# Attention values multiplied into the up weights batch by batch, nine rows to a partition, and stages interleaved by hand

## The chip, the cores and the metric

The kernel runs on one core of a Trainium2 chip. The metric is the device time of one execution in microseconds (us). Times of stretches and of single instructions come from one profiled execution, taken by the hardware profiler.

## What is computed

Eight batches of a memory attention, 8 heads of 576 tokens and 64 channels, with 32 memory slots a head, followed by a bilinear feed-forward layer over all 4608 tokens (512 channels, 1536 hidden). Cut to what matters:

```python
a = exp(phi - max(phi, axis=2)); a = a / (sum(a, axis=2) + 1e-09)
k_m = einsum('bhsm,bhsd->bhmd', a, k)
v_m = einsum('bhsm,bhsd->bhmd', a, v)
scores = matmul(q, k_m.transpose(0, 1, 3, 2)) / sqrt(64)
attn = softmax(scores, axis=-1)
x = matmul(attn, v_m).transpose(0, 2, 1, 3).reshape(4608, 512)
out = ((x @ w_a) * (x @ w_b)) @ w_out
```

All inputs are float32 in HBM, and so is the output.

## The kernel before

`attention_load(b)` (line 99) loads one batch in five chunks of 128 tokens (the last has 64), each chunk with the tokens on the partitions. phi comes over SP's queue (L113), q, k and v over POOL's queue (L115 to L117), which turns them into float16 on the way; a run in HBM is one token of one head, 64 numbers of q, k or v or 32 of phi. ACT takes the exponential of phi (L120), TensorE transposes q (L124, tile pqTc). Then, for two groups `g` of four heads, TensorE sums exp(phi) times k, v and a column of eights into pkvm (L138), 32 columns of the array to a head, and transposes the key part (L151).

`attention_tail(b)` (line 159) works in blocks of 288 tokens: the scores of four heads in four tiles of the array, 64 rows by 32 columns each (pscore, L168), exponential on ACT (L176), softmax denominators by a matmul with a block matrix (pD, L178), their reciprocals on DVE (L184, two halves of 144, for each block and group), the product (L185), and the values, poutT (L199), copied into `xT_sb`, the attention output of all tokens with the 512 channels on partitions.

`ffn(tbs)` (line 213) takes one or two blocks of 512 tokens. For each of 12 slices of the hidden width it sums four matmuls of 128 x 128 by 512 columns into pa and four into pb (L221), copies pa out on ACT or DVE (L231, L233), and multiplies by pb on DVE (L235). Then po (L240) sums 12 matmuls for each chunk of 128 tokens, which is copied out (L249, L251) and stored over SP's queue (L253).

The order of calls at the end of the function is attention(0), the loads of w_a and w_b (L90, L91), attention(1), attention(2), the load of w_out (L95), ffn([0]), and so on; a scheduler that goes by priorities and the readiness of data moves instructions within it, so attention work of later batches stands between pa and pb matmuls.

Of the kernel before, what the change touches and what calls it, by code (L numbers as in the profile page):

```python
# [8 lines left out]
F32 = mybir.dt.float32  # L10
F16 = mybir.dt.float16
AF = mybir.ActivationFunctionType
ALU = mybir.AluOpType


@with_exitstack
def kernel(
# [11 lines left out]
    nc = tc.nc  # L29
# [3 lines left out]
    d_model, d_ff = moe_w_a.shape  # L33
    T = out.shape[0]

    P = 128
    n_ch = (S + P - 1) // P
    ch_sz = [min(P, S - P * c) for c in range(n_ch)]
    SBK = 288
    n_sbk = S // SBK  # L40
    n_dm = d_model // P
    n_ffc = d_ff // P
    TBLK = 512
    n_tblk = T // TBLK
    KVW = 2 * D + 4
    inv_sqrt_d = 1.0 / float(D) ** 0.5

    consts = ctx.enter_context(tc.tile_pool(name="consts", bufs=1))
    persist = ctx.enter_context(tc.tile_pool(name="persist", bufs=1))
    a_in = ctx.enter_context(tc.tile_pool(name="a_in", bufs=6))  # L50
    ph_pool = ctx.enter_context(tc.tile_pool(name="ph_pool", bufs=3))
    kv_pool = ctx.enter_context(tc.tile_pool(name="kv_pool", bufs=3))
    a_bb = ctx.enter_context(tc.tile_pool(name="a_bb", bufs=3))
    ffn_hp = ctx.enter_context(tc.tile_pool(name="ffn_hp", bufs=3))
    ffn_op = ctx.enter_context(tc.tile_pool(name="ffn_op", bufs=3))
    ps_kvm = ctx.enter_context(tc.tile_pool(name="ps_kvm", bufs=1, space=bass.MemoryType.PSUM))
    ps_rot = ctx.enter_context(tc.tile_pool(name="ps_rot", bufs=3, space=bass.MemoryType.PSUM))
    ps_ab = ctx.enter_context(tc.tile_pool(name="ps_ab", bufs=2, space=bass.MemoryType.PSUM))

    ident16 = consts.tile([P, P], F16, name="ident16")  # L60
    make_identity(nc, ident16)
    blk32 = consts.tile([P, P], F16, name="blk32")
    nc.vector.memset(blk32, 0.0)
    nc.gpsimd.affine_select(
        out=blk32,
        in_=blk32,
        compare_op=ALU.is_gt,
        fill=0.125,
        base=1 - M,
        pattern=[[-M, P // M], [0, M]],  # L70
        channel_multiplier=1,
    )
    nc.gpsimd.affine_select(
        out=blk32,
        in_=blk32,
        compare_op=ALU.is_ge,
        fill=0.0,
        base=0,
        pattern=[[-M, P // M], [0, M]],
        channel_multiplier=1,  # L80
    )

    wa_sb = persist.tile([P, n_dm, d_ff], F16, name="wa_sb")
    wb_sb = persist.tile([P, n_dm, d_ff], F16, name="wb_sb")
    wout_sb = persist.tile([P, n_ffc, d_model], F16, name="wout_sb")
    xT_sb = persist.tile([P, n_dm, T], F16, name="xT_sb")

    def load_weights_ab():
        for c in range(n_dm):
            nc.gpsimd.dma_start(out=wa_sb[:, c, :], in_=moe_w_a[c * P:(c + 1) * P, :])  # L90
            nc.gpsimd.dma_start(out=wb_sb[:, c, :], in_=moe_w_b[c * P:(c + 1) * P, :])  # L91

    def load_weights_out():
        for i in range(n_ffc):
            nc.gpsimd.dma_start(out=wout_sb[:, i, :], in_=moe_w_out[i * P:(i + 1) * P, :])  # L95

    state = {}

    def attention_load(b):
        exp_phi = ph_pool.tile([P, n_ch, H, M], F16, name="exp_phi")  # L100
        qT_sb = a_bb.tile([P, n_dm, S], F16, name="qT_sb")
        kvm_sb = a_bb.tile([P, 2, 2 * D + 1], F16, name="kvm_sb")
        rphi_sb = a_bb.tile([P, 2], F32, name="rphi_sb")
        kmT_sb = a_bb.tile([P, 2, P], F16, name="kmT_sb")
        E_sb = a_bb.tile([P, 2, n_sbk, SBK], F16, name="E_sb")
        kv_b = kv_pool.tile([P, n_ch, H, KVW], F16, name="kv_b")
        state[b] = (qT_sb, kvm_sb, rphi_sb, kmT_sb, E_sb)

        for c in range(n_ch):
            cs = ch_sz[c]  # L110
            s0 = c * P
            phi_ch = a_in.tile([P, H, M], F32, name="phi_ch")
            nc.sync.dma_start(out=phi_ch[:cs], in_=phi[b, :, s0:s0 + cs, :].transpose([1, 0, 2]))  # L113
            q_ch = a_in.tile([P, H, D], F16, name="q_ch")
            nc.gpsimd.dma_start(out=q_ch[:cs], in_=q[b, :, s0:s0 + cs, :].transpose([1, 0, 2]))  # L115
            nc.gpsimd.dma_start(out=kv_b[:cs, c, :, 0:D], in_=k[b, :, s0:s0 + cs, :].transpose([1, 0, 2]))  # L116
            nc.gpsimd.dma_start(out=kv_b[:cs, c, :, D:2 * D], in_=v[b, :, s0:s0 + cs, :].transpose([1, 0, 2]))  # L117
            nc.vector.memset(kv_b[:cs, c, :, 2 * D:2 * D + 1], 8.0)

            nc.scalar.activation(out=exp_phi[:cs, c], in_=phi_ch[:cs], func=AF.Exp)  # L120

            pqTc = ps_rot.tile([P, n_dm, P], F16, name="pqTc", tag="ps_rot")
            for hp in range(n_dm):
                nc.tensor.transpose(  # L124
                    out=pqTc[:, hp, 0:cs],
                    in_=q_ch[:cs, 2 * hp:2 * hp + 2, :],
                    identity=ident16[0:cs, 0:cs],
                    tile_position=(0, 0),
                )
            nc.scalar.copy(out=qT_sb[:, :, s0:s0 + cs], in_=pqTc[:, :, 0:cs])  # L130

        for g in range(2):
            pkvm = ps_kvm.tile([P, KVW], F32, name="pkvm", tag="pkvm")
            for c in range(n_ch):
                cs = ch_sz[c]
                for j in range(4):
                    h = 4 * g + j
                    nc.tensor.matmul(  # L138
                        pkvm[32 * j:32 * (j + 1), 0:2 * D + 1],
                        exp_phi[:cs, c, h, :],  # L140
                        kv_b[:cs, c, h, 0:2 * D + 1],
                        start=(c == 0),
                        stop=(c == n_ch - 1),
                        tile_position=(0, 32 * j),
                    )
            nc.scalar.copy(out=kvm_sb[:, g, :], in_=pkvm[:, 0:2 * D + 1])  # L146
            nc.vector.reciprocal(out=rphi_sb[:, g:g + 1], in_=kvm_sb[:, g, 2 * D:2 * D + 1])  # L147

            pkmT = ps_rot.tile([P, P], F16, name="pkmT", tag="ps_rot")
            for half in range(2):  # L150
                nc.tensor.transpose(  # L151
                    out=pkmT[64 * half:64 * half + 64, :],
                    in_=kvm_sb[:, g, 0:D],
                    identity=ident16[:, :],
                    tile_position=(0, 64 * half),
                )
            nc.scalar.copy(out=kmT_sb[:, g, :], in_=pkmT)

    def attention_tail(b):
        qT_sb, kvm_sb, rphi_sb, kmT_sb, E_sb = state.pop(b)  # L160
        for g in range(2):
            for sb in range(n_sbk):
                pscore = ps_rot.tile([P, SBK], F32, name="pscore", tag="ps_rot")
                for j in range(4):
                    h = 4 * g + j
                    hp = h // 2
                    po2 = 64 * (h % 2)
                    nc.tensor.matmul(  # L168
                        pscore[32 * j:32 * (j + 1), :],
                        kmT_sb[po2:po2 + 64, g, 32 * j:32 * (j + 1)],  # L170
                        qT_sb[po2:po2 + 64, hp, sb * SBK:(sb + 1) * SBK],
                        start=True,
                        stop=True,
                        tile_position=(po2, 32 * j),
                    )
                nc.scalar.activation(out=E_sb[:, g, sb, :], in_=pscore, func=AF.Exp, scale=rphi_sb[:, g:g + 1])  # L176
                pD = ps_rot.tile([P, SBK], F32, name="pD", tag="ps_rot")
                nc.tensor.matmul(pD, blk32, E_sb[:, g, sb, :], start=True, stop=True, tile_position=(0, 0))  # L178
                recipD_sb = a_in.tile([P, SBK], F16, name="recipD_sb")
                HB = SBK // 2  # L180
                for hhh in range(2):
                    sl = slice(hhh * HB, (hhh + 1) * HB)
                    with nc.allow_low_precision("softmax denom reciprocal in fp16 is fine"):
                        nc.vector.reciprocal(out=recipD_sb[:, sl], in_=pD[:, sl])  # L184
                    nc.vector.scalar_tensor_tensor(  # L185
                        out=E_sb[:, g, sb, sl],
                        in0=E_sb[:, g, sb, sl],
                        scalar=rphi_sb[:, g:g + 1],
# [115 lines left out]
```

## Time and profile before

| | |
|---|---|
| median of 3 runs | 418.93 us (418.82 to 419.03) |
| span of the profiled execution | 416.7 us |
| TensorE busy | 346.5 us, 2096 matmuls |
| DVE / ACT / POOL busy | 204.9 / 111.8 / 112.6 us |
| read from HBM, written | 42.47 MB, 9.44 MB |
| mean granted TensorE clock | 0.975 |

PE is TensorE, PEld its weight loads, DVE the vector engine, ACT the scalar engine, POOL and SP the engines that here mostly issue transfers. A row of the groups gives line, engine, operation, output and inputs, count, then busy time and mean duration of one in ns, then the idle time before it and what ended it. Rows of the chain give start, duration and what the program waited for or did; rows of the timeline give start, duration, engine and instruction, with equal neighbours merged. The 40 slices of the page are 10.4 us each. The last two columns of the windows table are the busy share of the DMA engines and GB/s by bytes landed.

### The profile page before, as it was taken

How to read it: one execution, taken by the hardware profiler on the slowest of the kernel's cores; microseconds unless marked ns; L12 is line 12 of the kernel's file. 1: busy time of each engine (PE TensorE's matmuls, PEld its weight loads, DVE VectorE, ACT ScalarE, POOL GpSimd, SP SyncE). 2: the span in 40 equal slices, each digit the busy share in tenths (PEclk: the TensorE clock that was granted, in tenths of full speed). 3: DMA queues.
4: the chain of work that ended last, by engine and by line, in shares of the span. 5: the costliest groups of instructions: out<-in, count | busy, mean ns of one | idle time of the engine just before them, and what ended most of it. 6: DMA issues, size and time to landing. Idle time of an engine off the chain costs nothing.

```text
span 416.7 us, 5430 instructions
## 1 busy us (share of the span) xinstructions
PE 346.5 (83%) x2096; PEld 152.9 (37%) x2096; DVE 204.9 (49%) x391; ACT 111.8 (27%) x255; POOL 112.6 (27%) x148
## 2 busy tenths in 40 slices
PE   0200357994789999999999989999899999999996
PEld 0100113341234444344444434444344444444442
DVE  0000254773551898861198895116965512555411
ACT  3201424562432334311325321115311111111110
POOL 9544526796986913000302000000000000000000
PEclk9999996998689999999999999999999999999999
DMA  9999999999999969002471500220000022000022
GB/s 128 147 200 192 146 146 79 175 187 147 139 154 189 154 39 58 2 0 102 114 46 11 36 0 2 76 101 27 0 2 1 0 102 101 2 0 0 2 101 101
DMA packets 158105, 33.38 MB, mean 80 GB/s; under 512 B 150912, under 2 KB 152448, under 8 KB 158080
## 3 DMA queue, kind: packets, MB, share of 16 engines
q0 software_dynamic: 115392, 18.88, 60.7%
q1 hardware_dynamic: 42688, 14.16, 18.1%
q8 instruction: 16, 0.26, 0.2%
q14 instruction: 9, 0.07, 0.1%
HBM read 42.47 MB, written 9.44 MB: 125 GB/s over the span
## 4 chain that ended last, share of the span: by engine, by line
PE 75%; DMA 13%; ACT 3%; DVE 3%; issue 2%; POOL 1%; SPq 0%; DVEq 0%; POOLq 0%
PE po L240 23%; PE pa L221 22%; PE pb L221 21%; DMA phi_ch<-in_phi_dram 11%; DMA kv_b<-in_v_dram 2%; PE poutT L199 2%; PE pqTc L124 2%; DVE recipD_sb L184 2%; PE pD L178 1%; PE pkvm L138 1%; ACT h_sb L231 1%; PE pscore L168 1%; ACT xT_sb L209 1%; DVE E_sb L185 1%; POOL kv_b L116 1%
## 5 line engine op out<-in xcount | busy, mean ns | idle before, releaser
L221 PE MATMUL pa<-xT_sb,wa_sb 128*128 128x512 f16 x432 | 116.4, 386 | 4.1 <-ACT h_sb L231 3.9
L221 PE MATMUL pb<-xT_sb,wb_sb 128*128 128x512 f16 x432 | 113.1, 385 | 0.0
L240 PE MATMUL po<-wout_sb,h_sb 128*128 128x512 f16 x432 | 96.0, 383 | 0.0
L235 DVE TENSOR_TENSOR h_sb<-h_sb,pb 128x512 f16<-128x512 f16 x108 | 70.7, 681 | 37.0 <-PE pb L221 35.2
L184 DVE RECIPROCAL recipD_sb<-pD 128x144 f16<-128x144 f32 x64 | 63.0, 1026 | 24.6 <-PE pD L178 24.3
L231 ACT CAST h_sb<-pa 128x512 f16<-128x512 f32 x60 | 35.2, 586 | 136.1 <-PE pa L221 136.1
L240 PEld LDWEIGHTS <-h_sb 128*128 128x128 f16 x432 | 42.6, 99 | 52.0 <-issue 2.2
L221 PEld LDWEIGHTS <-wa_sb 128*128 128x128 f16 x432 | 40.9, 99 | 51.2 <-issue 7.2
L115 POOL DMA_DIRECT2D q_ch<-in_q_dram x40 | 34.0, 862 | 94.0 <-PE pqTc L124 84.4
L221 PEld LDWEIGHTS <-wb_sb 128*128 128x128 f16 x432 | 41.2, 98 | 46.9 <-issue 4.2
L251 DVE COPY o_sb<-po 128x512 f32<-128x512 f32 x18 | 12.4, 691 | 78.8 <-PE po L240 78.8
L233 DVE CAST h_sb<-pa 128x512 f16<-128x512 f32 x48 | 33.0, 688 | 19.9 <-PE pa L221 19.8
L116 POOL DMA_DIRECT2D kv_b<-in_k_dram x40 | 35.3, 883 | 7.5 <-DMA wb_sb<-in_moe_w_b_dram 2.4
L124 PE MATMUL pqTc<-ident,q_ch 128*128 128x128 f16 (+1 forms) x160 | 14.6, 233 | 27.3 <-ACT qT_sb L130 18.0
L117 POOL DMA_DIRECT2D kv_b<-in_v_dram x40 | 35.3, 883 | 5.8 <-DMA q_ch<-in_q_dram 2.8
L249 ACT COPY o_sb<-po 128x512 f32<-128x512 f32 x18 | 10.5, 586 | 77.9 <-PE po L240 77.9
L138 PE MATMUL pkvm<-kv_b,exp_phi 128*32 128x129 f16 (+1 forms) x320 | 15.1, 237 | 17.3 <-DMA kv_b<-in_v_dram 16.1
L120 ACT ACTIVATE exp_phi<-phi_ch 128x256 f16<-128x256 f32 (+1 forms) x40 | 15.2, 413 | 37.1 <-DMA phi_ch<-in_phi_dram 37.1
L147 DVE RECIPROCAL rphi_sb<-kvm_sb 128x1 f32<-128x1 f16 x16 | 1.9, 152 | 43.6 <-ACT kvm_sb L146 43.6
L130 ACT COPY qT_sb<-pqTc 128x512 f16<-128x512 f16 (+1 forms) x40 | 19.3, 550 | 14.4 <-PE pqTc L124 14.3
L124 PEld LDWEIGHTS <-q_ch 128*128 128x128 f16 (+1 forms) x160 | 10.8, 105 | 33.1 <-issue 19.9
L138 PEld LDWEIGHTS <-exp_phi 128*32 128x32 f16 (+1 forms) x320 | 7.5, 96 | 34.0 <-issue 22.5
(28 smaller groups left out, 129.4 us busy)
## 6 DMA issues: line engine op xcount, KB each, us to landing
out_dram<-o_sb SPq DMA_DIRECT2D x36, 256.0 KB, 2.0
phi_ch<-in_phi_dram SPq DMA_DIRECT2D x32, 128.0 KB, 8.1
q_ch<-in_q_dram POOLq DMA_DIRECT2D x32, 128.0 KB, 4.7
kv_b<-in_k_dram POOLq DMA_DIRECT2D x32, 128.0 KB, 6.2
kv_b<-in_v_dram POOLq DMA_DIRECT2D x32, 128.0 KB, 6.8
wa_sb<-in_moe_w_a_dram POOLq DMA_DIRECT2D x4, 384.0 KB, 11.0
wb_sb<-in_moe_w_b_dram POOLq DMA_DIRECT2D x4, 384.0 KB, 11.7
wout_sb<-in_moe_w_out_dram POOLq DMA_DIRECT2D x12, 128.0 KB, 5.9
```

The costliest lines, as they stand in the source:

```text
L115: nc.gpsimd.dma_start(out=q_ch[:cs], in_=q[b, :, s0:s0 + cs, :].transpose([1, 0, 2]))
L116: nc.gpsimd.dma_start(out=kv_b[:cs, c, :, 0:D], in_=k[b, :, s0:s0 + cs, :].transpose([1, 0, 2]))
L117: nc.gpsimd.dma_start(out=kv_b[:cs, c, :, D:2 * D], in_=v[b, :, s0:s0 + cs, :].transpose([1, 0, 2]))
L124: nc.tensor.transpose(out=pqTc[:, hp, 0:cs], in_=q_ch[:cs, 2 * hp:2 * hp + 2, :], identity=ident16[0:cs, 0:cs], tile_position=(0, 0),)
L130: nc.scalar.copy(out=qT_sb[:, :, s0:s0 + cs], in_=pqTc[:, :, 0:cs])
L138: nc.tensor.matmul(pkvm[32 * j:32 * (j + 1), 0:2 * D + 1], exp_phi[:cs, c, h, :], kv_b[:cs, c, h, 0:2 * D + 1], start=(c == 0), stop=(c == ...
L184: nc.vector.reciprocal(out=recipD_sb[:, sl], in_=pD[:, sl])
L221: nc.tensor.matmul(pzs[ti], w_sb[:, c, i * P:(i + 1) * P], xT_sb[:, c, tbs[ti] * TBLK:(tbs[ti] + 1) * TBLK], start=(c == 0), stop=(c == n_ ...
L231: nc.scalar.copy(out=h_sbs[ti][:, i, :], in_=pas[ti])
L233: nc.vector.tensor_copy(out=h_sbs[ti][:, i, :], in_=pas[ti])
L235: nc.vector.tensor_tensor(out=h_sbs[ti][:, i, :], in0=h_sbs[ti][:, i, :], in1=pbs[ti], op=ALU.mult)
L240: nc.tensor.matmul(po, h_sbs[ti][:, i, jj * P:(jj + 1) * P], wout_sb[:, i, :], start=(i == 0), stop=(i == n_ffc - 1),)
```

## The change

The kernel is rewritten around the same mathematics. Parts:

1. **Values into the weights.** The attention output x is no longer formed. With A the softmax weights (32 slots x 8 heads = 256 rows by 576 tokens) and V the value memory of one batch, x W = A^T (V W). For every batch the kernel computes V W for both up weights (tiles `vab`, PSUM tile `pva`, L245): 48 matmuls of 64 x 32 weights by 512 columns, four heads in four tiles of the array. The up projection then contracts over 256 rows: per batch, slice and half of the tokens two matmuls of 288 columns into pa (L317) and two into pb (L326).
2. **Nine rows to a partition.** q, k, v and phi of a batch come in one transfer each, all on POOL's queue. A partition holds nine consecutive tokens of a head, one run of 576 numbers (288 of phi). Two heads share the 128 partitions, so the sums over tokens (pkv, L159) run with 64 rows, nine matmuls a head, 192 columns each: k, v and a third block of eights. Softmax denominators of both groups and both halves go to one tile (pD, L214), reciprocals are taken once per batch (2 x 144), and a small matmul spreads them again (pR, L228).
3. **Hand-ordered interleaving.** No scheduler moves instructions: every engine works in the order of the code. `up(b)` emits batch b's up projection; after each half slice `advance` pumps two generators, first `down` of the batch before (2 or 3 matmuls), then 1 or 2 steps of `attention(b + 1)`. Loads for batch b + 2 are issued ahead of `up(b)`. The first attention and the last five output chunks stand alone.

```diff
+    def rows(x, b):
+        return x[b].rearrange("h s d -> (h s d)").rearrange("(c p f) -> p c f", c=NHP, p=P)
-            nc.sync.dma_start(out=phi_ch[:cs], in_=phi[b, :, s0:s0 + cs, :].transpose([1, 0, 2]))
-            nc.gpsimd.dma_start(out=q_ch[:cs], in_=q[b, :, s0:s0 + cs, :].transpose([1, 0, 2]))
...
+        nc.gpsimd.dma_start(out=phi_sb, in_=rows(phi, b))
...
+        nc.gpsimd.dma_start(out=q_sb, in_=rows(q, b))
...
+    ctx.enter_context(tc.manual_schedule())
+    load_kv(0)
+    load_q(0)
+    load_wab(0)
...
+    load_wab(1)
+    load_wab(2)
+    load_kv(1)
+    load_q(1)
+    for n in range(3):
+        load_wo(n)
...
+        for n in range(NCH):
+            for z in range(2):
+                for g in range(2):
+                    pva = ps_at.tile([P, 512], F32, name="pva", tag="at")
+                    for j in range(4):
+                        r, hp = j % 2, 2 * g + j // 2
+                        nc.tensor.matmul(
+                            pva[32 * j:32 * j + 32, :],
+                            kvT[64 * r:64 * r + 64, g, 1, M * j:M * j + M],
+                            w_sbs[z][64 * r:64 * r + 64, hp, 512 * n:512 * (n + 1)],
...
+                    if e % 2:
+                        nc.vector.tensor_copy(out=dst, in_=pva)
                     else:
+                        nc.scalar.copy(out=dst, in_=pva)
+                    e += 1
+                    yield
...
+        def advance(x):
+            done[0] += side_rate * x
+            done[1] += work_rate * x
...
+            pump(work, n1)
+            pump(side, n0)
+
+        for i in range(NFF):
...
+            for hf in range(2):
+                pa = ps_up.tile([P, HALF], F32, name="pa")
+                for g in range(2):
+                    nc.tensor.matmul(pa, vab[0][:, g, fs], A[:, g, HALF * hf:HALF * (hf + 1)],
+                                     start=(g == 0), stop=(g == 1))
...
+                nc.scalar.copy(out=a_sb, in_=pa)
+            advance(0.5)
+            for hf in range(2):
+                pb = ps_up.tile([P, HALF], F32, name="pb")
...
+                nc.vector.tensor_tensor(out=ht[:, i, t0:t0 + HALF], in0=a_sbs[hf], in1=pb, op=ALU.mult)
+            advance(0.5)
...
+        if b + 2 < B:
+            load_kv(b + 2)
+            load_q(b + 2)
+        side = attention(b + 1) if b + 1 < B else nothing
+        ready = (S * b) // P
+        work = chain([down(c) for c in range(next_chunk, ready)])
...
+        up(b, side, work, n_side / NFF, n_work / NFF)
```

PSUM is divided into two buffers each for pa, pb and po, and two (`ps_at`) that all tiles of `attention` share in turn. Outputs are stored 64 partitions at a time, two transfers a chunk.

TensorE before, in a stretch where attention work of a later batch stands in the up projection (pscore are scores, pa and pb the up projection, pD the denominators):

```order
L168 MATMUL pscore<-qT_sb,kmT_sb 32x288 [waits PE_49]
...
L221 LDWEIGHTS wa_sb
L221 MATMUL pa<-xT_sb,wa_sb 128x512 [waits Activation_49]
L221 LDWEIGHTS wb_sb
L221 MATMUL pb<-xT_sb,wb_sb 128x512 [waits DVE_49]
...
L178 LDWEIGHTS blk_93
L178 MATMUL pD<-E_sb,blk_93 128x288 [waits Activation_49]
```

TensorE now, at the same place of a batch (vab are the products of values and weights, A the softmax weights, ht the hidden layer, po the down projection, rD the reciprocals):

```order
L270 MATMUL po<-wo_sb,ht 128x512
L198 LDWEIGHTS kvT
L198 MATMUL pscore<-qT,kvT 32x256 [waits Activation_49]
...
L214 MATMUL pD<-E,sel 32x288 [waits Activation_49]
...
L326 MATMUL pb<-A,vab_2763 128x288 [waits DVE_49]
...
L270 LDWEIGHTS ht
L270 MATMUL po<-wo_sb,ht 128x512
L228 LDWEIGHTS spread [waits DVE_49]
L228 MATMUL pR<-rD,spread 128x288 [waits PE_49]
```

pD now follows the last scores directly, with no up matmuls between, and pR comes after one half step of pb and po; before, up matmuls stood between the scores and pD.

POOL's queue before, from the last chunk of batch 0 (64 tokens) to the up weights:

```order
L115 DMA q_ch<-in_q_dram 64x8x64
L116 DMA kv_b<-in_k_dram 64x8x64
L117 DMA kv_b<-in_v_dram 64x8x64
L90 DMA wa_sb<-in_moe_w_a_dram 128x1536
L91 DMA wb_sb<-in_moe_w_b_dram 128x1536
```

POOL's queue now, from its first transfer:

```order
L81 DMA phi_sb<-in_phi_dram 128x4x288
L83 DMA kv_sb_93<-in_k_dram 128x4x576
L84 DMA kv_sb_93<-in_v_dram 128x4x576
L89 DMA q_sb<-in_q_dram 128x4x576
L94 DMA wa_sb<-in_moe_w_a_dram 128x4x512
L95 DMA wb_sb<-in_moe_w_b_dram 128x4x512
```

Batch 0 is four transfers in place of twenty, phi has come from SP's queue to this one, and the up weights come in thirds of their columns; the other two thirds stand ahead of batch 1, and w_out behind it.

More of the change, by code (lines that the diff above doesn't have):

```diff
@@ L13 @@
 ALU = mybir.AluOpType
+P = 128
+CS = 16.0
 @with_exitstack
@@ L51 @@
[L51 to L95, printed above, removed]
@@ new lines, with load_kv @@
+    w_sbs = (wa_sb, wb_sb)
+    def rows(x, b):
+        return x[b].rearrange("h s d -> (h s d)").rearrange("(c p f) -> p c f", c=NHP, p=P)
+    inputs = {}
+    kv_sbs = [consts.tile([P, 3, NHP, NI * D], F16, name=f"kv_sb{t}") for t in range(2)]
+    for t in range(2):
+        nc.vector.memset(kv_sbs[t][:, 2], 8.0)
+    def load_kv(b):
+        phi_sb = inp.tile([P, NHP, NI * M], F32, name="phi_sb")
+        nc.gpsimd.dma_start(out=phi_sb, in_=rows(phi, b))
+        kv_sb = kv_sbs[b % 2]
+        nc.gpsimd.dma_start(out=kv_sb[:, 0], in_=rows(k, b))
+        nc.gpsimd.dma_start(out=kv_sb[:, 1], in_=rows(v, b))
+        inputs[b] = [phi_sb, kv_sb]
@@ new lines, in load_q, with load_wab, load_wo @@
+    def load_q(b):
+        q_sb = inp.tile([P, NHP, NI * D], F16, name="q_sb")
+        nc.gpsimd.dma_start(out=q_sb, in_=rows(q, b))
+        inputs[b].append(q_sb)
+    def load_wab(n):
+        sl = slice(512 * n, 512 * (n + 1))
+        nc.gpsimd.dma_start(out=wa_sb[:, :, sl], in_=wa_rows[:, :, sl])
+        nc.gpsimd.dma_start(out=wb_sb[:, :, sl], in_=wb_rows[:, :, sl])
+    def load_wo(n):
+        sl = slice(4 * n, 4 * (n + 1))
+        nc.gpsimd.dma_start(out=wo_sb[:, sl, :], in_=wo_rows[:, sl, :])
@@ L138, in attention_load @@
                     nc.tensor.matmul(
[L139 to L171, printed above, removed]
+                        ps[32 * j:32 * j + 32, 0:n, :],
@@ L178, in attention_tail @@
[L178 to L188, printed above, removed]
-                        in1=recipD_sb[:, sl],
-                        op0=ALU.mult,
-                        op1=ALU.mult,
-                    )
@@ L193, in attention_tail @@
-                for hh in range(2):
-                    hp = 2 * g + hh
-                    poutT = ps_rot.tile([P, SBK], F32, name="poutT", tag="ps_rot")
-                    for pp in range(2):
-                        hq = 2 * hp + pp
-                        j = hq % 4
+                nc.scalar.activation(out=Ev[:, g, 0:n, par, :], in_=ps[:, 0:n, :], func=AF.Exp,
+                                     scale=rphi[:, g:g + 1])
+                yield
+        pD = ps_at.tile([P, HALF], F32, name="pD", tag="at")
@@ new lines, in attention @@
+        for g in range(2):
+            for hf in range(2):
+                t = 2 * g + hf
+                nc.tensor.matmul(pD[32 * t:32 * t + 32, :], sel, E[:, g, HALF * hf:HALF * (hf + 1)],
+                                 start=True, stop=True, tile_position=(0, 32 * t))
+        rD = mid.tile([P, HALF], F16, name="rD")
+        for z in range(2):
+            sl = slice(z * HALF // 2, (z + 1) * HALF // 2)
+            with nc.allow_low_precision("softmax denominators"):
+                nc.vector.reciprocal(out=rD[:, sl], in_=pD[:, sl])
@@ new lines, in attention @@
+        yield
+        A = mid.tile([P, 2, S], F16, name="A")
+        for g in range(2):
+            for hf in range(2):
+                t = 2 * g + hf
+                pR = ps_at.tile([P, HALF], F32, name="pR", tag="at")
+                nc.tensor.matmul(pR, spread[32 * t:32 * t + 32, :], rD[32 * t:32 * t + 32, :],
+                                 start=True, stop=True, tile_position=(32 * t, 0))
+                sl = slice(HALF * hf, HALF * (hf + 1))
+                nc.vector.scalar_tensor_tensor(out=A[:, g, sl], in0=E[:, g, sl], scalar=rphi[:, g:g + 1],
+                                               in1=pR, op0=ALU.mult, op1=ALU.mult)
+                yield
@@ L199, in attention_tail @@
+        attn[b] = A
+        vab = [mid.tile([P, 2, d_ff], F16, name=f"vab{z}") for z in range(2)]
+        vabs[b] = vab
+        e = 0
+        for n in range(NCH):
+            for z in range(2):
+                for g in range(2):
+                    pva = ps_at.tile([P, 512], F32, name="pva", tag="at")
+                    for j in range(4):
+                        r, hp = j % 2, 2 * g + j // 2
                         nc.tensor.matmul(
-                            poutT[64 * pp:64 * pp + 64, :],
@@ new lines, in attention, with down @@
+                    e += 1
+                    yield
+    hts = {}
+    out_rows = out.rearrange("(b p i) f -> b i p f", b=B, i=NI)
+    def down(cidx):
+        pair, c = divmod(cidx, NI)
+        ht = hts[pair]
+        po = ps_dn.tile([P, d_model], F32, name="po")
+        for i in range(NFF):
+            nc.tensor.matmul(po, ht[:, i, P * c:P * (c + 1)], wo_sb[:, i, :],
+                             start=(i == 0), stop=(i == NFF - 1))
+            if i < NFF - 1:
+                yield
+        o_sb = opool.tile([P, d_model], F32, name="o_sb")
+        if cidx % 2:
+            nc.vector.tensor_scalar(out=o_sb, in0=po, scalar1=1.0 / (CS * CS), scalar2=None, op0=ALU.mult)
+        else:
+            nc.scalar.mul(out=o_sb, in_=po, mul=1.0 / (CS * CS))
+        for z in range(2):
+            slot = 2 * c + z
+            nc.sync.dma_start(out=out_rows[2 * pair + slot // NI, slot % NI], in_=o_sb[64 * z:64 * z + 64, :])
+        yield
@@ new lines @@
+    nothing = iter(())
+    gens = {b: attention(b) for b in range(1)}
+    for _ in gens[0]:
+        pass
+    n_side = 40
+    next_chunk = 0
+    for b in range(B):
+        if b + 2 < B:
[4 more added lines that the diff above has]
+        work = chain([down(c) for c in range(next_chunk, ready)])
+        n_work = (ready - next_chunk) * (NFF + 0)
+        next_chunk = ready
+        up(b, side, work, n_side / NFF, n_work / NFF)
+        for _ in work:
+            pass
+        for _ in side:
+            pass
@@ L277 @@
+    for c in range(next_chunk, T // P):
+        for _ in down(c):
+            pass
 _INS = ['q', 'k', 'v', 'phi', 'moe_w_a', 'moe_w_b', 'moe_w_out']
```

240 lines of the change are left out of this document (127 added, 113 removed).

## Prediction

> **What bounds the kernel now.** I read the page first, then the chain of waits in order of time, then stretches of the timeline.
>
> ```profile
> PE 346.5 (83%) x2096; PEld 152.9 (37%) x2096; DVE 204.9 (49%) x391; ACT 111.8 (27%) x255; POOL 112.6 (27%) x148
> PE   0200357994789999999999989999899999999996
> DMA  9999999999999969002471500220000022000022
> DMA packets 158105, 33.38 MB, mean 80 GB/s; under 512 B 150912, under 2 KB 152448, under 8 KB 158080
> ```
> A slice is 10.4 us. TensorE is nearly idle in the first four slices while the DMA engines are full, and is full from about slice 12 on. So there are two stages with different limits, and the chain names them:
>
> ```profile
> 2.59 39.03 DMA phi_ch<-in_phi_dram x4
> 205.18 0.78 PE pqTc L124 x12
> 350.53 1.73 PE pa L221 x8
> 391.97 20.73 PE po L240 x96
> 412.79 0.69 DVE o_sb L251
> ```
> The first 41.6 us wait for loads. Late in the program eight 512-column matmuls take 1.73 us, 216 ns each, and 96 take 20.73: one column per 0.42 ns, with nothing between. The last output leaves TensorE at 412.79, and 3.9 us later the span of 416.7 ends. The median of the runs, 418.93, lies 2.2 us above that span; I add 2.2 at the end.
>
> **Up and down projections.** Per batch before: up is 2 x 12 x 4 passes over 576 tokens, 55,296 columns; down is 12 passes of 512 columns for each of 4.5 chunks, 27,648 columns. The change contracts over 256 (8 heads x 32 memory slots) in place of 512, so up halves to 96 matmuls of 288 columns. What such a matmul takes, and what a tiled group costs between full matmuls, stands in one stretch of TensorE's timeline:
>
> ```profile
> 211.29 0.59 PE L221 MATMUL pa<-xT_sb,wa_sb 128*128 128x512 f16 x2
> 211.81 0.32 PE L199 MATMUL poutT<-E_sb,kvm_sb 32*64 32x288 f16 x4
> 212.06 0.30 PE L168 MATMUL pscore<-qT_sb,kmT_sb 64*32 64x288 f16 x4
> 212.34 0.38 PE L221 MATMUL pa<-xT_sb,wa_sb 128*128 128x512 f16 x1
> 212.56 1.02 PE L221 MATMUL pb<-xT_sb,wb_sb 128*128 128x512 f16 x4
> 213.42 0.29 PE L178 MATMUL pD<-E_sb,blk 128*128 128x288 f16 x1
> 213.54 0.38 PE L221 MATMUL pb<-xT_sb,wb_sb 128*128 128x512 f16 x1
> ```
> The single pD of 288 columns holds the array from 213.42 to 213.54: 0.12 us, its weight load hidden. Up now takes 96 x 0.122 = 11.75 us a batch; before it was 96 x 576/512 x 0.216 = 23.3. Down stays at 54 x 0.216 = 11.65. So 8 x 11.6 = 92 us of TensorE goes.
>
> **The tiled groups.** Four pscore matmuls (64 rows x 32 columns) last 0.30 us together where the single pD lasts 0.29: they run at once. The added product of V and the up weights uses the same four tile positions, 48 matmuls of 512 columns a batch in 12 groups: 12 x 0.216 = 2.6 us. The value and key sums become 72 matmuls of 192 columns in 18 rounds of 0.08: 1.44 us. Transposes: 20 at 0.065 (0.78/12) and 8 small ones: 1.6 us. The rest (four score groups, pD, four pR) is 0.5 + 0.1 + 0.5. Sum 6.7 us a batch.
>
> Changing the tile shape costs. pscore to pa is 0.28 us for 0.12 of streaming, poutT to pscore 0.25, and poutT starts 0.09 after the pa before it has streamed (211.29 + 2 x 0.216 = 211.72). So 0.09 to go in and 0.12 to 0.16 to come out, 0.22 to 0.25 an excursion. The order of the changed kernel has 18 excursions a batch: 18 x 0.235 = 4.2 us. This is the rule of the Trainium skill, TensorEngine Tiling (Array Packing), Key Properties, that changing the tiling mode drains TensorE; it speaks against interleaving. The page gives no price for it, so the sum goes by the row; were switches free, stages 1 to 6 would be 25 us shorter together.
>
> **Waits of TensorE on its own side work.** The order is written by hand and TensorE works in order, so a side step that waits holds the up and down matmuls behind it. Other durations:
>
> ```profile
> L231 ACT CAST h_sb<-pa 128x512 f16<-128x512 f32 x60 | 35.2, 586 | 136.1 <-PE pa L221 136.1
> L233 DVE CAST h_sb<-pa 128x512 f16<-128x512 f32 x48 | 33.0, 688 | 19.9 <-PE pa L221 19.8
> L235 DVE TENSOR_TENSOR h_sb<-h_sb,pb 128x512 f16<-128x512 f16 x108 | 70.7, 681 | 37.0 <-PE pb L221 35.2 <-ACT qT_sb L130 1.4 <-ACT h_sb L231 0.3
> L211 DVE CAST xT_sb<-poutT 128x288 f16<-128x288 f32 x32 | 13.1, 451 | 3.7 <-PE poutT L199 3.7
> L209 ACT CAST xT_sb<-poutT 128x288 f16<-128x288 f32 x32 | 11.2, 401 | 15.2 <-PE poutT L199 15.1
> L184 DVE RECIPROCAL recipD_sb<-pD 128x144 f16<-128x144 f32 x64 | 63.0, 1026 | 24.6 <-PE pD L178 24.3
> L176 ACT ACTIVATE E_sb<-pscore,rphi_sb 128x288 f16<-128x288 f32 x32 | 16.3, 509 | 10.9 <-PE pscore L168 10.6
> ```
> From 451 to 688 ns, 224 more elements cost DVE 237 ns, so a product of 288 takes 681 - 237 = 444 ns and a copy of 1024 about 1.23 us. DVE per batch: 24 products 10.7, six vab copies 4.1, three qT copies 3.15, two reciprocals 2.05 (eight before), four A steps 1.8, outputs 1.5, kvm 0.6: 23.9 us. ACT: 24 copies 9.6, six vab copies 3.5, exponentials 3.5, the rest 1.9: 18.5. Neither is the bound at 34 us or more of TensorE; what counts is where a step comes due too early.
>
> Each half step of the order has 4 up matmuls (0.49 us), 2 or 3 down (0.43 to 0.65), then one or two side steps. Walked through:
> - kvm's transposes need the buffer of the second q transpose, whose two 1.23 us copies run in turn: 2.65 us after the first transpose, due after about 1.95. Wait 0.7.
> - The first score needs the third qT copy, which stands behind two products of 0.44: 0.35.
> - pD needs the fourth exponential, which on ACT stands behind two 0.40 us copies of pa: due after 0.2, ready after 1.4. Wait 1.2.
> - pR needs both reciprocals, 0.29 + 2 x 1.026 after pD; 1.15 to 1.35 of it is covered by up and down. Wait 1.1.
> - vab: its two PSUM buffers are emptied in turn by ACT and DVE, 0.6 to 0.7 each plus about 0.9 of queue, and come round after 1.5 or more. I take 0.
>
> Sum 3.35 us. A stage with all three kinds of work is 11.75 + 11.65 + 6.7 + 4.2 + 3.35 = 37.7 us. Ends: 34.3 without the waits; with the waits doubled and as much again on vab, 44.5.
>
> **Loads.** Packets of 128 bytes become runs of 576 elements (1152 bytes in f16).
>
> ```profile
> 0.00:20.00 20.00, 3.30 (x28) 1.80 (x28) 0.45 (x11) 5.92 (x12) 15.36 (x26) 1.00 1.75 137
> 25.00:35.00 10.00, 0.00 (x0) 0.00 (x0) 0.00 (x0) 0.00 (x0) 4.33 (x6) 1.00 1.16 216
> 80.00:89.00 9.00, 9.00 (x78) 3.64 (x76) 7.52 (x19) 5.79 (x15) 6.67 (x11) 1.00 1.34 202
> out_dram<-o_sb SPq DMA_DIRECT2D x36, 256.0 KB, 2.0
> ```
> The last column is GB/s by bytes landed: 137 with short runs, 216 while the 3 KB weight rows came in, 202 while 1 KB rows of w_out did, the latter two with phi beside them. I take 180 for 1152 alone (ends 137 and 216). A batch is 2.36 MB, 13.1 us; a third of wa and wb 1.05 MB, 5.8; w_out 1.57 MB, 8.7. Data from 2.6 us on (the chain's first row), seen about 1.5 after the last byte (an estimate from the 2.0 us row, which holds the issue as well): q of batch 0 at 17.2, the last third of wa and wb at 34.6, v of batch 1 at 44.4, its q at 47.7, batch 2 at 69.5. Later a stage brings 2.36 MB and sends 1.18: 19.7 us of 37.7, so loads stay ahead.
>
> - Start: from q at 17.2, transposes and copies to 21, kvT 21.8, scores 24, reciprocals 26.3, A 28.5, eight vab groups at 0.5 to 32.5, the last four after 34.6: **36.6 us**.
> - Stage 0: after one step, batch 1's sums stand in TensorE's queue and hold batch 0's up matmuls until v at 44.4, its transposes until q at 47.7. Then DVE has 20 us left (23.9 without outputs, four products and kvm) and idles about 3.5 around the exponentials: ends at 71.2, **34.6 us**. (With 216 GB/s q lands at 40.5, with 137 at 61.5: -7 and +14.)
> - Stages 1 to 6: 6 x 37.7 = **226.2**.
> - Stage 7, no side work: 11.75 + 48 x 0.216 = **22.1**.
> - Tail: five chunks, 60 x 0.216 = 12.9, plus the 3.9 seen now: **16.9**.
>
> 36.6 + 34.6 + 226.2 + 22.1 + 16.9 = 336.4 of span, 338.6 with the 2.2: I say 339.
>
> **The rivals.**
> 1. *The waits are covered or switches cheaper.* Six stages at 34.3: 318; if switches also cost nothing, 30.1, and 293. For it: products on other engines can drift ahead. Against it: pD and pR wait on chains that start only one half step earlier. The 318 lies in my range; below 312, chance 0.08.
> 2. *Row tiles of one bank take turns.* The four matmuls of a group write one PSUM bank from two row groups. If those alternated, a group would take two rounds: 2.6 + 1.44 + 0.5 more, 4.5 us a batch, 7 batches on the path: 370. The 0.30 us of pscore, same positions and one bank, speaks against it. The Trainium skill, TensorEngine Tiling (Array Packing), Gotcha 1: PSUM Pressure, says that different row tiles cannot access the same bank at once; the trace disagrees at 288 columns, and no run yet shows 512. Chance 0.06, inside the range.
> 3. *In-order waits are several times my walk* (vab and products shutting each other out of two buffers): stages at 44 to 50, 376 to 412. For it: ps_at has two buffers for all side work, and a late DVE holds products and side steps alike. Chance 0.11.
> 4. *Slower than before*: a group runs its four matmuls one after another, because each waits on its own weight load. vab 10.35 for 2.6, sums 5.8 for 1.44, the rest 1.8 more: 13.9 a batch, 8 x 13.9 = 111, giving 450. The change loses once stages 1 to 6 pass (418.9 - 2.2 - 36.6 - 34.6 - 22.1 - 16.9)/6 = 51 us each. Against it: 0.30 for four. Chance 0.03.
>
> **How the numbers follow.** My own case has 0.72. Its range takes load rates from 137 to 216 (-7 to +14) and stages of 34.3 to 44.5 (-20 to +41). Downward I take both, 312; upward the larger alone, 380, since late loads and long waits hardly come together. Rival 2 lies inside. Left out are 0.08 below and, above, most of rival 3 and rival 4, 0.12. About 0.2% is what a measurement of this kernel can tell from no change. Faster by more: 0.95, within: 0.01, slower: 0.04 (rival 4, and 0.01 for the far end of rival 3).
>
> **What would show it.** Up matmuls 0.12 apart; pva groups about 0.45 from the po before to the pb behind; TensorE idle before pD and pR of about 1 us once a batch; batch 0's up held by loads of batch 1 until 44 to 48; stages 1 to 6 near 38 us each. It is wrong if groups of pva take over 0.4 of streaming, if loads are still waited for after 70 us, or if DVE is named most in TensorE's waits with over 6 us a stage.

## The result, and the profile after

The changed kernel takes 323.71 us (median of 4 runs, 323.3 to 324.07) where the kernel before takes 418.88 on the same chip: a ratio of 0.7732, 95% interval 0.7721 to 0.7743. The profiled execution has a span of 321.8 us.

The head of the page after, with the slices (8.0 us each now):

```profile
PE 285.2 (89%) x2576; PEld 147.5 (46%) x2576; DVE 170.0 (53%) x350; ACT 131.3 (41%) x315; POOL 33.0 (10%) x53
PE   0438697999899989999899989999899989999994
PEclk9985587899999999999799999999999999999999
DMA  7999999948612692149512691111102111112144
DMA packets 24367, 33.46 MB, mean 104 GB/s; under 512 B 1808, under 2 KB 18704, under 8 KB 24336
```

The same bytes now come in 24,367 packets where there were 158,105. TensorE is nearly full from slice 9 on. In slices 4 to 8 it is full in part only (8, 6, 9, 7, 9 tenths) and below full clock: the clock row says 5, 5, 8, 7, 8 there.

Cut at the first pa of each batch, the span gives the stages of the forecast. The columns of the windows view are the stretch, its length, then busy time of TensorE, weight loads, DVE, ACT and POOL, the granted clock, the DMA share and GB/s:

```profile
33.00:67.30 34.30, 29.40 (x272) 14.93 (x269) 19.34 (x41) 14.96 (x37) 4.59 (x7) 0.77 1.18 220
67.30:101.50 34.20, 32.72 (x319) 17.07 (x317) 20.18 (x44) 16.19 (x40) 2.97 (x4) 1.00 0.47 94
101.50:138.40 36.90, 35.49 (x329) 18.18 (x328) 21.23 (x46) 15.89 (x39) 2.99 (x4) 1.00 0.51 101
245.10:282.00 36.90, 35.49 (x329) 18.20 (x328) 21.32 (x46) 15.90 (x39) 0.00 (x0) 1.00 0.16 37
282.00:304.10 22.10, 22.10 (x145) 14.09 (x144) 10.79 (x26) 9.38 (x26) 0.00 (x0) 1.00 0.21 49
304.10:321.80 17.70, 13.16 (x61) 5.78 (x59) 2.53 (x5) 1.79 (x3) 0.00 (x0) 1.00 0.39 89
```

| part | forecast, us | measured, us |
|---|---|---|
| start, to batch 0's first up matmul | 36.6 | 33.0 |
| stage 0 | 34.6 | 34.3 |
| stages 1 to 6 | 226.2 (37.7 each) | 214.7 (34.2 to 37.0, mean 35.8) |
| stage 7, no side work | 22.1 | 22.1 |
| tail | 16.9 | 17.7 |
| span | 336.4 | 321.8 |

TensorE's own waits after (us in total, number, longest):

```profile
PE pkv L159 <- DMA kv_sb<-in_v_dram: 14.4, 2, 12.0
PE pR L228 <- DVE rD L220: 9.2, 8, 2.2
PE pD L214 <- ACT E L206: 3.6, 8, 0.7
PE pva L245 <- DVE vab L255: 0.6, 2, 0.3
```

Beside the loads of the first two batches only the two waits at the denominators are of any size, and they come back with every batch: in stages 1 to 6 TensorE waits 0.45 us before pD and 0.8 to 1.0 before pR. They and the groups around them stand in this stretch of TensorE's timeline, in stage 3:

```profile
151.53 0.29 PE L198 MATMUL pscore<-qT,kvT 64*32 64x256 f16 x4
151.75 0.30 PE L214 MATMUL pD<-E,sel 128*32 128x288 f16 x2
152.50 0.30 PE L214 MATMUL pD<-E,sel 128*32 128x288 f16 x2 [0.45 <-ACT E L206]
152.73 0.67 PE L326 MATMUL pb<-A,vab 128*128 128x288 f16 x4
153.23 0.59 PE L270 MATMUL po<-wo_sb,ht 128*128 128x512 f16 x2
154.86 0.41 PE L228 MATMUL pR<-rD,spread 32*128 32x288 f16 x1 [1.03 <-DVE rD L220]
155.21 1.14 PE L317 MATMUL pa<-A,vab 128*128 128x288 f16 x4
159.94 0.59 PE L270 MATMUL po<-wo_sb,ht 128*128 128x512 f16 x2
160.46 0.40 PE L245 MATMUL pva<-wa_sb,kvT 64*32 64x512 f16 x4
160.79 0.67 PE L326 MATMUL pb<-A,vab 128*128 128x288 f16 x4
```

Four pva matmuls last 0.40 us together; the two po ahead of them, 0.216 apart, last 0.59, so 0.38 for one. The four run at once. From the po stream's end (159.94 + 2 x 0.216 = 160.37) to the pb behind is 0.42 us, of which 0.216 is streaming: 0.20 us for going in and coming out. After the idle time before pR the four pa take 1.14 us in place of 0.67: the array ran at half rate for a while (mean granted clock 0.61 from 154 to 158 us).

### The profile page after: what moved, and what is told of

Same layout as the page of the kernel before. It is cut to its first block, busy times and chain, and to the rows that moved or that the text cites. A ratio compares the mean times of both kernels' runs of the same rounds, so it can differ in the third digit from the quotient of the medians.

```text
span 321.8 us, 6497 instructions
## 1 busy us (share of the span) xinstructions
PE 285.2 (89%) x2576; PEld 147.5 (46%) x2576; DVE 170.0 (53%) x350; ACT 131.3 (41%) x315; POOL 33.0 (10%) x53
## 2 busy tenths in 40 slices
DMA packets 24367, 33.46 MB, mean 104 GB/s; under 512 B 1808, under 2 KB 18704, under 8 KB 24336
## 4 chain that ended last, share of the span: by engine, by line
PE 78%; DMA 10%; DVE 5%; ACT 3%; issue 3%; POOL 1%; DVEq 0%; POOLq 0%
PE po L270 27%; PE pb L326 17%; PE pa L317 15%; PE pva L245 8%; DMA kv_sb<-in_v_dram 6%; PE pkv L159 4%; DMA wa_sb<-in_moe_w_a_dram 4%; PE pqT L151 2%; DVE rD L220 2%; PE pR L228 2%; ACT E L206 1%; ACT a_sb L320 1%; PE pscore L198 1%; DVE ht L329 1%; DVE o_sb L276 1%
## 5 line engine op out<-in xcount | busy, mean ns | idle before, releaser
L270 PE MATMUL po<-wo_sb,ht 128*128 128x512 f16 x432 | 121.1, 380 | 0.0
L329 DVE TENSOR_TENSOR ht<-a_sb,pb 128x288 f16<-128x288 f16 x192 | 78.1, 446 | 59.9 <-PE pb L326 55.1
L320 ACT CAST a_sb<-pa 128x288 f16<-128x288 f32 x192 | 67.8, 405 | 80.0 <-PE pa L317 79.6
L326 PE MATMUL pb<-A,vab 128*128 128x288 f16 x384 | 65.8, 295 | 0.1
L317 PE MATMUL pa<-A,vab 128*128 128x288 f16 x384 | 65.6, 295 | 0.0
L270 PEld LDWEIGHTS <-ht 128*128 128x128 f16 x432 | 42.4, 98 | 19.8
L255 DVE CAST vab<-pva 128x512 f16<-128x512 f32 x48 | 33.2, 691 | 33.4 <-PE pva L245 33.1
L257 ACT CAST vab<-pva 128x512 f16<-128x512 f32 x48 | 28.2, 587 | 48.7 <-PE pva L245 48.7
L326 PEld LDWEIGHTS <-vab 128*128 128x128 f16 x384 | 33.4, 100 | 27.8 <-issue 12.6
L317 PEld LDWEIGHTS <-vab 128*128 128x128 f16 x384 | 32.9, 99 | 27.6 <-issue 12.7
L159 PE MATMUL pkv<-kv_sb,exp_sb 64*32 64x192 f16 x576 | 18.4, 270 | 14.4 <-DMA kv_sb<-in_v_dram 14.4
L159 PEld LDWEIGHTS <-exp_sb 64*32 64x32 f16 x576 | 12.9, 102 | 23.5 <-issue 20.9
L245 PEld LDWEIGHTS <-kvT 64*32 64x32 f16 x384 | 7.8, 91 | 28.2 <-issue 27.3
L245 PE MATMUL pva<-wb_sb,kvT 64*32 64x512 f16 x192 | 19.4, 420 | 0.9 <-DVE vab L255 0.3
L245 PE MATMUL pva<-wa_sb,kvT 64*32 64x512 f16 x192 | 19.2, 419 | 0.7 <-DVE A L231 0.2
L228 PE MATMUL pR<-rD,spread 32*128 32x288 f16 x32 | 8.6, 327 | 10.2 <-DVE rD L220 9.2
```

The lines of the kernel that those rows point to most:

```text
L159: nc.tensor.matmul(pkv[32 * j:32 * j + 32, g, :], exp_sb[64 * r:64 * r + 64, hp, i, :], kv_sb[64 * r:64 * r + 64, :, hp, D * i:D * (i + 1) ...
L245: nc.tensor.matmul(pva[32 * j:32 * j + 32, :], kvT[64 * r:64 * r + 64, g, 1, M * j:M * j + M], w_sbs[z][64 * r:64 * r + 64, hp, 512 * n:51 ...
L255: nc.vector.tensor_copy(out=dst, in_=pva)
L257: nc.scalar.copy(out=dst, in_=pva)
L270: nc.tensor.matmul(po, ht[:, i, P * c:P * (c + 1)], wo_sb[:, i, :], start=(i == 0), stop=(i == NFF - 1))
L317: nc.tensor.matmul(pa, vab[0][:, g, fs], A[:, g, HALF * hf:HALF * (hf + 1)], start=(g == 0), stop=(g == 1))
```

## The experiments

One theory stood against two rivals. *Work*: in stages 1 to 6 TensorE's instructions set the time, so each part is worth what it takes off TensorE or what it covers there, and long runs count only until batch 1 has arrived. The rivals: that the loads bring most, or that the hand order brings most, with the fold no more than paying for its own 48 matmuls and 12 copies. Then the disputed prices, one by one. The kernel before, run beside them, took 418.01 us (first four) and 418.23 (last four).

**The fold undone (e1_no_fold).** 390.4 us; ratio to before 0.9335 (0.9319 to 0.9352).

```diff
-                        nc.tensor.matmul(pva[32 * j:32 * j + 32, :], kvT[...], w_sbs[z][...], ...)
+                    nc.tensor.matmul(pX[64 * r:64 * r + 64, :], kvm[32 * j:32 * j + 32, hp // 2, D:2 * D],
+                                     A[32 * j:32 * j + 32, hp // 2, sl], ...)
...
-                for g in range(2):
-                    nc.tensor.matmul(pa, vab[0][:, g, fs], A[:, g, HALF * hf:HALF * (hf + 1)],
+                for hp in range(NHP):
+                    nc.tensor.matmul(pa, wa_sb[:, hp, fs], vab[:, hp, HALF * hf:HALF * (hf + 1)],
```

> The fold undone alone: x is formed per batch (16 matmuls of 288 columns, eight copies), and up contracts over 512 rows again, 192 matmuls a batch. Theory 'work' (TensorE's own work in stages 1 to 6 sets the time, and halving up is the largest part): a stage gains 11.7 us of up and 2.8 of x and loses 4.2 of pva, +10.3; six stages +62, stage 0 +8, stage 7 +11.7, start -4: about 400 us. Rival 'order' (the loads and the hand order bring most of the gain, the fold pays for itself with its own 48 matmuls and 12 copies): 345 us or less.

66.7 us more than with the fold, so the rival is out, though the time is some 10 us under the expected 400. Stages 1 to 6 take 43.1 to 45.5 us, 8.5 us more on average (50.9 together); stage 7 takes 33.9 (+11.8), stage 0 40.5 (+6.2), the start 31.2 (-1.8). The stage is 1.8 us cheaper than expected, in part because its half steps are longer and cover more of the waits before the spreading matmul, 5.8 us in all where the kernel with the fold has 9.2:

```profile
PE pR L228 <- DVE rD L220: 5.8, 8, 2.2
```

Another 0.25 us a stage is a spell at half clock in one stage of the changed kernel (see the last section); the rest of the 1.8 is not accounted for. Without the fold the kernel is still 27.6 us faster than the kernel before: that is what the other parts bring together when there is no fold.

**Long runs undone (e2_short_runs).** 334.41 us; ratio 0.7997 (0.7970 to 0.8025).

```diff
-        nc.gpsimd.dma_start(out=kv_sb[:, 0], in_=rows(k, b))
...
+        for t, x in ((0, k), (1, v)):
+            for c in range(NHP):
+                nc.gpsimd.dma_start(out=kv_sb[:, t, c, :, 0:D], in_=rows(x, b)[:, c])
```

> Long runs undone alone: the same bytes to the same places, but q, k, v and phi come in runs of 64 (phi 32) numbers, 128 bytes landed, in several transfers of one partition set each. Theory 'work': loads fall from 207 to about 145 GB/s, batch 1's q lands about 10 us later, stages 1 to 6 stay near 36 us since 2.4 MB at 145 GB/s is 16 us: 334 us. Rival 'loads' (long runs bring most of the gain, the DMA engines bound the program again as in the first 150 us of before): 370 us or more, with stages 1 to 5 over 42.

10.7 us more. In the profiled executions the start is 7.8 us longer and stage 0 3.4, all that follows 0.1: long runs matter until stage 1 and not after. The windows of the first 20 us, of after and of this kernel:

```profile
0.00:20.00 20.00, 5.94 (x116) 4.66 (x117) 6.26 (x9) 4.54 (x8) 12.14 (x25) 1.00 1.01 184
```
```profile
0.00:20.00 20.00, 3.59 (x72) 2.86 (x73) 4.69 (x6) 2.65 (x3) 18.87 (x25) 1.00 1.39 110
```

184 GB/s became 110, and POOL is busy 18.87 us of the 20. The chain of this kernel gives the first 20 us to POOL issuing transfers:

```profile
1.33 4.13 POOL phi_sb L82 x4
5.47 7.96 POOL kv_sb L86 x8
13.43 4.76 POOL q_sb L94 x6
```

So the chain puts the price of the first batch on issuing its 20 transfers (the kernel before had as many, five of them on SP's queue), at 0.8 to 1.1 us each, rather than on moving the short packets. The time came out as expected, by another limit than the one named. As this run has both more transfers and shorter runs in each, it does not show what short runs in four transfers would cost.

**The interleaving of attention undone (e3_side_first).** 386.51 us; ratio 0.9240 (0.9209 to 0.9271).

```diff
+        for _ in side:
+            pass
         up(b, side, work, n_side / NFF, n_work / NFF)
```

> The interleaving of attention undone alone: attention(b + 1) is emitted whole ahead of batch b's up projection; down stays between the up matmuls. Theory 'work': the chain of attention stands open, some 15 to 20 us in which TensorE works 7; a stage becomes 39 to 43 us, total 345 to 373. Rival 'order': the hand order brings most, 390 us or more. If the order brings nothing: 324.

62.8 us more, 13.5 above the upper end that the theory gave and 3.5 below where the rival began, so this run alone does not decide between them; the rival's other half, that the fold only pays for itself, fell with the fold undone. The chain of attention alone took about 19 us in a stage, and in it TensorE lost its clock (78 to 96 us):

```profile
78.00:96.00 18.00, 11.69 (x97) 3.64 (x95) 9.45 (x15) 6.08 (x12) 1.70 (x3) 0.66 0.71 128
```

Its timeline shows the longest stop in that chain, and what the fall of the clock costs behind it:

```profile
84.89 0.42 PE L228 MATMUL pR<-rD,spread 32*128 32x288 f16 x2 [2.06 <-DVE rD L220]
95.05 1.14 PE L317 MATMUL pa<-A,vab 128*128 128x288 f16 x4
95.99 1.06 PE L270 MATMUL po<-wo_sb,ht 128*128 128x512 f16 x2
97.60 0.59 PE L270 MATMUL po<-wo_sb,ht 128*128 128x512 f16 x2
```

The granted clock over those 18 us is 0.66, and the first po pair behind takes 1.06 us where the next takes 0.59. Seven such chains cost 9.0 us each where the theory had 3 to 7. Its price left the clock out; how much of the excess the clock makes was not separated. This and the first experiment's 66.7 us together exceed the 95 us that the change gained: each is what the kernel loses without one part while the others stay, so the two are not shares of the gain. The kernel before interleaved attention as well, by its scheduler, and no run has the fold under that scheduler. What the order by hand is worth against the scheduler's stays open.

**The two waits taken away (e4_spaced).** 310.75 us; ratio 0.7426 (0.7410 to 0.7441): 13.0 us faster than the changed kernel.

```diff
+        yield
         pD = ps_at.tile([P, HALF], F32, name="pD", tag="at")
...
                 nc.vector.reciprocal(out=rD[:, sl], in_=pD[:, sl])
         yield
+        yield
+        yield
```

> Three empty steps added: the denominators come a half step after the last scores, the spreading matmul one or two half steps after the reciprocals. Theory 'waits' (TensorE's two waits of about 0.6 and 1.1 us a stage are real stalls of the in-order queue): -1.7 us in each of six stages and in stage 0, about 312 us. Rival: the wait only moves to the pva groups, which now come later and closer: 322 us or more.

The waits were real stalls, and little took their place:

```profile
PE pR L231 <- DVE rD L221: 3.5, 4, 2.2
PE pR L231 <- DVE A L234: 1.6, 4, 0.7
PE pva L248 <- DVE vab L258: 0.6, 2, 0.3
PE pD L215 <- ACT E L206: 0.4, 2, 0.3
```

9.2 us before pR became 3.5, 3.1 of them in the start and stage 0; 3.6 before pD became 0.4; those before pva stayed at 0.6, and waits of pR for the product A of the softmax weights rose from 0.7 to 1.6. Stages 1 to 6 take 32.9 to 35.2 us (204.5 together, 10.2 less), stage 0 31.5 (2.8 less). Of the 10.2, 1.5 are a spell at half clock in stage 3 of the changed kernel (see the last section), which this execution did not have.

**The price of a change of tile shape (e5_switch) and its control (e6_same_shape).** 329.22 us, ratio 0.7868 (0.7837 to 0.7898), and 323.67 us, ratio 0.7740 (0.7700 to 0.7780). Both add matmuls whose results are overwritten.

```diff
                 pa = ps_up.tile([P, HALF], F32, name="pa")
+                if b == B - 1 and hf == 0:
+                    for j in range(4):
+                        r = j % 2
+                        nc.tensor.matmul(pa[32 * j:32 * j + 32, 0:64], wa_sb[64 * r:64 * r + 64, j, 0:32],
+                                         wb_sb[64 * r:64 * r + 64, j, 0:64], start=True, stop=True,
+                                         tile_position=(64 * r, 32 * j))
```

> Stage 7 alone, which has no side work, gets a group of four tiled matmuls (64 rows x 32 columns, 64 columns streamed, results overwritten) at the start of each of its 24 half steps. Theory 'switch' (going into a tiled shape and out of it costs about 0.2 us a time, as the rows of after show): 24 x (0.20 + 0.03) = +5.5 us in stage 7 and in the time, 329 us. Rival 'free' (the gaps seen around pva groups come from their waits, not from the shape): +24 x 0.03 to 0.06, 325 us or less.

> The control: in the same 24 places one matmul of the full 128 x 128 shape over 64 columns. Both theories: +24 x 0.03 to 0.06 us, 324.5 to 325.2 us. If it costs as much as the tiled group, the price is not that of the shape.

5.55 us between the two in the medians. The control's time is that of the changed kernel (323.71), and its four runs spread over 3.1 us, so the cost of its one full matmul is read from the timeline alone. Stage 7's timeline, first with the tiled group, then with the one full matmul:

```profile
283.58 0.59 PE L270 MATMUL po<-wo_sb,ht 128*128 128x512 f16 x2
284.11 0.21 PE L334 MATMUL pb<-wb_sb,wa_sb 64*32 64x64 f16 x4
284.25 0.66 PE L338 MATMUL pb<-A,vab 128*128 128x288 f16 x4
284.75 0.59 PE L270 MATMUL po<-wo_sb,ht 128*128 128x512 f16 x2
```
```profile
283.47 0.59 PE L270 MATMUL po<-wo_sb,ht 128*128 128x512 f16 x2
283.90 0.19 PE L318 MATMUL pa<-wb_sb,wa_sb 128*128 128x64 f16 x1
283.93 0.66 PE L321 MATMUL pa<-A,vab 128*128 128x288 f16 x4
284.42 0.59 PE L270 MATMUL po<-wo_sb,ht 128*128 128x512 f16 x2
```

From po to po is 1.17 us with the tiled group and 0.95 with the full one, where up and down alone need 0.92: 0.25 against 0.03. Nothing waits there, so about 0.22 us is the price of going into the tiled shape and out of it. The group also has four weight loads where the control has one, and no control with four was run. A stretch of the changed kernel bounds what this difference in number can cost:

```profile
70.80 0.92 PE L159 MATMUL pkv<-kv_sb,exp_sb 64*32 64x192 f16 x36
71.65 0.66 PE L326 MATMUL pb<-A,vab 128*128 128x288 f16 x4
```

Nine rounds of four tiled matmuls, each with its own weight load, take 0.85 us up to the pb behind, 0.094 a round. The 64 columns of a group alone stream 0.027, so that it has four loads in place of one is worth at most 0.07 of the 0.22 (an estimate from these rows). Part of the price is cover that the loads lose: the control's weight load starts at 283.69, 0.21 us ahead of its matmul and under the po, those of the tiled group only at 284.11, together with its matmuls.

**Batch 1 held back in stage 0 (e7_late1).** 307.21 us; ratio 0.7357 (0.7321 to 0.7392), the fastest version tried.

```diff
         phi_sb, kv_sb, q_sb = inputs.pop(b)
+        if b == 1:
+            for _ in range(5):
+                yield
```

> The spaced kernel, with batch 1's attention held back by five empty steps in stage 0, so that batch 0's up matmuls run while batch 1's v is still on its way. Theory 'queue' (about 3 us of stage 0 are up matmuls held behind the sums that wait for v): stage 0 falls from 31.5 to about 29, total about 308 us. Rival: batch 1's chain then ends later and stage 0 with it: 311 us or more.

Stage 0 falls from 31.5 to 26.7 us, more than expected. Its first matmuls, from the first pa on:

```profile
33.58 1.14 PE L323 MATMUL pa<-A,vab 128*128 128x288 f16 x4
34.52 1.17 PE L332 MATMUL pb<-A,vab 128*128 128x288 f16 x4
35.48 1.08 PE L323 MATMUL pa<-A,vab 128*128 128x288 f16 x4
36.39 0.66 PE L332 MATMUL pb<-A,vab 128*128 128x288 f16 x4
37.63 0.59 PE L162 MATMUL pkv<-kv_sb,exp_sb 64*32 64x192 f16 x20
```

Up matmuls now fill the time until the sums start at 37.6, without a wait for v, and the clock is back by 36.4 (four pb in 0.66 us), where in the changed kernel TensorE waited for v and then worked at half clock until 42. The rival (batch 1's chain ends later) is out.

**One step to more half steps (e8_rate36).** 311.84 us; ratio 0.7460 (0.7434 to 0.7486).

```diff
-    n_side = 40
+    n_side = 36
```

> The spaced kernel, with 36 side steps in place of 40 handed out over the 24 half steps, so more half steps hold one step. Theory 'waits': the remaining waits before the spreading matmuls (about 0.9 us a stage in every second stage) shrink, while two or three more changes of tile shape at 0.2 us are added: 309 to 312 us. Rival: more than 313, if the changes of shape weigh more than the waits.

No gain over e4_spaced (310.75; the intervals overlap a little). Stages 1 to 6 take 33.3 to 35.5, 0.3 more each. The waits before pR that are left, 3.1 us in two places, lie in the start and in stage 0; in stages 1 to 6 e4_spaced had at most 0.4 us a stage left to gain there, not the 0.9 in every second stage that was expected. Each stage now goes into a tiled shape 20 times in place of 18, which at 0.22 us is 0.44: the added changes of shape took what the waits gave, and a little more. Start and stage 0 together are 64.9 us against 64.8, so nothing is gained there either.

## Why the prediction was right, step by step

The time lay inside the range and 4.5% under the forecast of 339; the mechanism was the one named. Rival 1 (the waits are covered, stages of 34.3) came about half true: stages 1 to 6 took 35.8 us on average, where the forecast had 37.7.

- *Up halves, 0.122 us a matmul.* Right: stage 7, which has up and down alone, takes 22.1 us as worked out, with TensorE busy for all of it. Undoing the fold cost 66.7 us.
- *Four tiles run at once; pva streams 0.216 a group.* Right; rivals 2 and 4 are out. The Trainium skill, TensorEngine Tiling (Array Packing), Gotcha 1: PSUM Pressure, says that different row tiles cannot access the same PSUM bank at once. The 0.40 us of four pva, two row groups and one bank, shows no turn-taking at 512 columns; each of the four had its own 32 partitions of the bank.
- *0.235 us an excursion.* Right in size: 0.20 in the timeline, 0.22 in e5_switch against its control, 17 of them a stage in the trace in place of 18. The rule of the Trainium skill, TensorEngine Tiling (Array Packing), Key Properties, that a change of tiling mode drains TensorE, agrees with these rows.
- *Waits of 3.35 us a stage.* Too large, and the largest miss of the sum: the windows show TensorE idle for 1.4 to 1.5 us of a stage, 1.9 less, as much as stages 1 to 6 came out shorter. pR waited 0.8 to 1.0 us, near the 1.1 of the forecast. pD waited 0.45 in place of 1.2: two of its four matmuls went ahead of the last exponential, and that was ready sooner (152.45 us, 0.9 after the last scores started, in place of 1.4). The two at the transposes and the first score (0.7 and 0.35) were not there, but for 0.16 in stage 3. They rested on qT copies of 1.23 us (two) and, by the 3.15 us for all three, 0.69, scaled from copies of float32 sources. The copy of 1024 numbers from a float16 tile took 686 ns, the third (512 numbers, 64 partitions) about 0.41 us:

```profile
L178 DVE COPY qT<-pqT 128x1024 f16<-128x1024 f16 x16 | 10.4, 686 | 5.4 <-PE pqT L151 5.3
```

- *Loads at 180 GB/s.* Too low: 207 in the rows below, near the upper end of the bounds. TensorE had q of batch 0 at 15.0 us in place of 17.2, and read the last third of the up weights from 30.2 on without a wait, where the forecast had it at 34.6. Hence the start of 33.0 in place of 36.6.
- *Stage 0 at 34.6.* The sum was right by two errors that cancel. v of batch 1 came at 37.5, not 44.4, so 4.5 us after the start of the stage in place of 7.8. Against that, the rest of the stage took 29.8 us in place of 26.8, as TensorE had the half clock for part of it, of which the working said nothing. The windows of after in the first 60 us (columns as above):

```profile
36.00:39.00 3.00, 1.51 (x23) 1.06 (x24) 0.00 (x0) 0.00 (x0) 0.74 (x1) 0.50 1.21 207
42.00:45.00 3.00, 2.98 (x45) 2.21 (x45) 2.45 (x7) 0.70 (x2) 0.74 (x1) 0.96 1.23 202
48.00:51.00 3.00, 1.53 (x13) 0.69 (x12) 1.34 (x2) 1.27 (x4) 0.74 (x1) 1.00 1.19 215
54.00:57.00 3.00, 3.00 (x16) 0.98 (x16) 1.40 (x4) 1.38 (x3) 0.00 (x0) 0.50 1.19 245
```

- *The other engines are not the bound.* Right: DVE is busy 20 to 21 us of a stage, and waits of TensorE for vab copies sum to under 1 us.
- *It is wrong if loads are waited for after 70 us.* They were not.

## What to carry to other kernels

Find the operand that a chain of matmuls shares and fold it into the smaller side: contracting over 256 in place of 512 was worth 67 us here, although the fold itself adds 48 matmuls a batch, because these are small enough to run four at a time. When one engine works through an order written by hand, walk the order with measured durations and look for a consumer that stands less than its producer's time behind it; three empty steps at two such places were worth 11 to 13 us. Take a copy's price from a row with the same source type, and count what an idle TensorE does to its clock.

## What the runs showed of the hardware

- The granted clock has two values in these rows, 1.00 and 0.50; means between them are taken as mixtures. It does not go by the load of the moment: from 48 to 51 us TensorE was busy for 1.53 of 3.00 us at a clock of 1.00, from 54 to 57 for all of it at 0.50. One spell began after a short stop: in stage 3, TensorE waited 1.03 us until 154.9, and some 3 us at half rate followed. The same wait in stages 1 and 5 was not followed by it, nor was that of stage 3 in e5_switch and e6_same_shape, where stage 3 has the same instructions and took 34.5 us in place of 36.0. So the spell cost 1.5 us; what decides whether it comes is not shown. The Trainium skill, TensorE: Matmul & The Clock Gate, Part 1: The HAM clock gate, describes a throttled state at half rate that activity releases; the rows agree with the two values.
- A DVE copy from a float16 tile in PSUM ran at about twice the speed per element of one from float32: 686 ns for 1024 against 691 for 512. The Trainium skill, VectorE: DVE Perf Modes, Why PSUM operands drop a tier, says that an operand in PSUM caps such an operation at double speed, and at single speed for fp32; these rows agree.
